# Attention of a three-stage kernel put in order by a list scheduler that models the program fetch

## The chip, the cores and the metric

The kernel runs on one core of a Trainium2 chip. A core has five engines with an instruction stream each: TensorE (PE) for matmuls, VectorE (DVE), ScalarE (ACT), GpSimd (POOL), and SyncE (SP), which here only issues DMAs. Each engine runs its own list in the order in which the program gives it, and waits at an instruction whose inputs or buffers are not ready. The metric is the device time of one execution in microseconds, the median over several runs: 375.57 us before the change (three runs, 374.45 to 375.98).

## The reference

Three layers follow one another. `S` is 576, `D` is 64; there are 4 batches and 8 heads.

```python
scores = scale * (q @ k.T)                        # per batch and head
mask   = local (0 <= i - j < 32)  for heads 0-3
         strided (i >= j, i % 32 == j % 32)  for heads 4-7
attn   = softmax(where(mask, scores, -1e9));  x = attn @ v      # 2304 tokens x 512
logits = x @ phi                                  # 8 experts x 4 slots
d = softmax of logits over tokens;  slot_in = d.T @ x
slot_out[e] = relu(slot_in[e] @ w1[e]) @ w2[e]    # w1 512x1024, w2 1024x512
y   = softmax of logits over slots @ slot_out
out = elu(y @ w_in) @ w_out                       # w_in 512x2048, w_out 2048x512, 8 bytes an element
```

## The kernel before

**Attention.** Both masks leave only small blocks, so attention is done in 20 units. A *local* unit (letter L, twelve of them, in two passes p = 0 and 1 over two heads each) takes a sixth of a pass: one bf16 product that writes the mask into PSUM, 24 small products of keys and queries on top of it, and 12 calls for the values that become 24 matmuls. A *strided* unit (letter S, eight of them, in passes p = 2 and 3) takes a quarter of a pass: a mask product, 32 calls that become 64 matmuls, and 16 calls for the values that become 32. Every matmul has a weight load of its own in front, and both are instructions of PE.

A unit goes through the engines like this: scores on PE (`emit_A`, L172 to L194), maximum and subtraction on DVE (L205, L206), exponential on ACT (`emit_E`, L214), sum, reciprocal, product and transpose on DVE (`emit_N`, L223 to L233), then four copies that spread the transposed blocks into the block-diagonal buffer `bd` (`spread`, L241 on ACT, L243 on POOL, L245 on DVE; the strings of `SPREAD` name the engine of each block), then the value products on PE and their copy to `x_all` on ACT (`emit_PV`, L262 to L281). When all units of a part of the tokens are through, `emit_X` multiplies them by `phi` (L291), transposes them (L298), adds to `logits` on DVE (L301, L303) and copies the transposes back on ACT (L308).

**What sets the order.** `ORDER` gives the sequence of units. A loop over `it` then emits, by hand, the normalisation of unit `it - 1`, the scores of unit `it`, the values of unit `it - 2`, the logits that the table `X_AT` puts there and the loads of the table `LOADS`. After the loop the tail is written out instruction by instruction: the last values, three soft-max steps over tokens (`emit_m`, `emit_mm`, `emit_ex`, `emit_dt`) and the accumulations `emit_acc` of slot inputs. Then come the first expert products (`emit_w1`, L581), the second ones (`emit_w2`, L671) and the MLP, whose operations were already put in order by a list scheduler with due times, written inline.

**Loads and slots.** All loads are issued by SP in program order. There is no room for all weights at once: first weights of experts 0 and 1 go to free slots, the others lie where queries, keys and values were and wait for their last reader. First weight 2 takes the values of pass 2, 3 the strided keys (`kB`), 4 the queries of passes 3 and 0, 5 the values of pass 3, 6 the local values, 7 the local keys (`kA`). Second weights 0 to 2 take `bd` and the two halves of `x_all`, the rest the slots of first weights that were used. `load_head` brings the first 256 columns of `w_in` early.

Of the kernel before, what the change touches and what calls it, by code (L numbers as in the profile page):

```python
# [19 lines left out]
def attn_moe_mlp(ctx, tc, q, k, v_l, v_s, phi, w1, w2, w_in, w_out, out):  # L20
# [18 lines left out]
    ORDER = "LLSLSSLSSLSSLSLLLLLL"  # L39
# [33 lines left out]
    def region(tag, name):  # L73
        return slots.tile([128, SIZE[tag]], F32, tag=tag, name=name)

# [72 lines left out]
    pend_S = []  # L148

# [7 lines left out]
    nth = [sum(y[0] // 2 == x[0] // 2 for y in units[:n]) for n, x in enumerate(units)]  # L157
    st = {}

# [5 lines left out]
    def emit_A(n):  # L165
        p, t, h = units[n]
        qt, kt = qk_t[p]
        if p < 2:
            u = 2 * t + h
            ps = s_ps[n % 2][:, 0:384].rearrange("p (a b) -> p a b", b=64)  # L170
            m0 = 0 if u == 0 else 1
            nc.tensor.matmul(  # L172
                s_ps[n % 2][:, 0:384], ident16, lmask16[:, m0:m0 + 3].rearrange("p i h x -> p (i h x)"),
                start=True, stop=False,
            )
            for j in range(3):
                i = 3 * u + j
                for b in range(B):
                    c0 = 128 * i + 32 * b
                    nc.tensor.matmul(  # L180
                        ps[32 * b:32 * b + 32, 2 * j:2 * j + 2, :], qt[:, c0:c0 + 32], kpair(p, i, b),
                        start=False, stop=(j == 2),
                    )
            s = small("s", 384, "ls", 3, 6, 64)
            ops_ = []
            w = 6
            pa = s
        else:
            ps = s_ps[n % 2][:, 0:16 * MR].rearrange("p (a b) -> p a b", b=MR)
            nc.tensor.matmul(s_ps[n % 2][:, 0:16 * MR], ident16, smask16, start=True, stop=False)  # L190
            for j in range(0, 16, 2):
                for b in range(B):
                    c0 = 576 * h + 288 * (j // 8) + B * MR * (j % 8 // 2) + b * MR
                    nc.tensor.matmul(  # L194
                        ps[32 * b:32 * b + MR, j:j + 2, :], qt[:, 1152 * t + c0:1152 * t + c0 + MR], kt[:, t, :, c0:c0 + MR],
                        start=False, stop=(j == 14),
                    )
            s = small("s", 16 * MR, "ss", 3, 16, MR)
            ops_ = []
            w = 16  # L200
            pa = pst[nth[n] % 2][:, :, 0:MR]
        sh = [128, w, s.shape[2]]
        mx = sl_p.tile([128, 16, 1], F32, tag="mx", name="mx", bufs=3)
        sc = ps
        ops_.append(lambda: nc.vector.reduce_max(out=mx[:, 0:w, 0], in_=sc, axis=AX.X))  # L205
        ops_.append(lambda: nc.vector.tensor_tensor(  # L206
            out=s, in0=sc, in1=mx[:, 0:w].to_broadcast(sh), op=ALU.subtract
        ))
        st[n] = [pa, w, sh, s]
        return ops_  # L210

    def emit_E(n):
        pa, s = st[n][0], st[n].pop()
        nc.scalar.activation(out=pa, in_=s, func=AF.Exp, scale=scale)  # L214

    def emit_N(n):
        p, t, h = units[n]
        pa, w, sh = st[n]
        sm = sl_p.tile([128, 16, 1], F32, tag="sm", name="sm", bufs=4)
        st[n].append(sm)  # L220
        sv = sm[:, 0:w]
        ops_ = [
            lambda: nc.vector.reduce_sum(out=sv[:, :, 0], in_=pa, axis=AX.X),  # L223
            lambda: nc.vector.tensor_scalar(out=sv, in0=sv, scalar1=1e-9, scalar2=None, op0=ALU.add),
            lambda: nc.vector.reciprocal(out=sv, in_=sv),
        ]
        bd = bds[n % 2]
        st[n].append(bd)
        ops_.append(lambda: nc.vector.tensor_tensor(out=pa, in0=pa, in1=sv.to_broadcast(sh), op=ALU.mult))
        r, x = (12, 32) if p < 2 else (16, MR)  # L230
        tr = small("pt", 32 * r, "tr", 2, r, 32)
        pin = pa.rearrange("p a (k x) -> p (a k) x", x=32) if p < 2 else pst[nth[n] % 2]
        ops_.append(lambda: nc.vector.transpose(out=tr, in_=pin))  # L233

        def spread():
            for b in range(B):
                q32 = slice(32 * b, 32 * b + 32)
                o, i = bd[q32, 0:r, 32 * b:32 * b + x], tr[q32, :, 0:x]
                e = SPREAD[1 if p >= 2 else 2 if n == nu - 1 else 0][b]
                if e == "A":  # L240
                    nc.scalar.activation(out=o, in_=i, func=AF.Copy)  # L241
                elif e == "G":
                    nc.gpsimd.tensor_copy(out=o, in_=i)  # L243
                else:
                    nc.vector.tensor_copy(out=o, in_=i)  # L245

        pend_S.append(spread)
        return ops_

    SPREAD = ("GAGA", "AAAA", "GAVA")  # L250
    nu = len(units)

    def emit_PV(n):
        p, t, h = units[n]
        pa, w, sh, sm, pt = st.pop(n)
        if p < 2:
            o = o_ps[nth[n] % 2][:, 0:384].rearrange("p (j x) -> p j x", x=128)
            for j in range(3):
                i = 3 * (2 * t + h) + j
                for k in range(2):  # L260
                    for e in range(2):
                        nc.tensor.matmul(  # L262
                            o[64 * e:64 * e + 64, j, :], v_t[p][:, max(i - 1 + k, 0), e, :], pt[:, 4 * j + 2 * e + k],
                            start=(k == 0), stop=(k == 1),
                        )
            i = 3 * (2 * t + h)
            nc.scalar.activation(out=x_all[:, POS[p], i:i + 3, :], in_=o, func=AF.Copy)
        else:
            xv = x_all[:, POS[p]].rearrange("p m (b q) -> p q b m", b=B)
            for g in range(2):  # L270
                og = ps_t.tile([128, 512], F32, tag="t", name="so")[:, 0:4 * B * MR]
                for j in range(4):
                    c0 = B * MR * j
                    r = 4 * g + j
                    for hh in range(2):
                        nc.tensor.matmul(
                            og[64 * hh:64 * hh + 64, c0:c0 + B * MR], v_t[p][:, t, h, hh, r, :],
                            pt[:, 8 * hh + r].rearrange("p (b m) -> p b m", b=B)[:, :, 0:MR], start=True, stop=True,
                        )
                q0 = 16 * t + 8 * h + 4 * g  # L280
                nc.scalar.activation(  # L281
                    out=xv[:, q0:q0 + 4], in_=og.rearrange("p (j b m) -> p j b m", b=B, m=MR), func=AF.Copy
                )

    seen = set()

    def emit_X(p, t):
        xt = x_all[:, POS[p], 6 * t:6 * t + 6, :]
        lg = ps_l.tile([128, 192], F32, tag="l", name="lg")
        for b in range(B):  # L290
            nc.tensor.matmul(  # L291
                lg[32 * b:32 * b + 32, :], phi_sb[:, p, :], xt[:, :, 32 * b:32 * b + 32], start=True, stop=True
            )
        xps = []
        for g in range(2):
            xps.append(ps_t.tile([128, 3, 128], F32, tag="t", name="xtps"))
            for j in range(3):
                nc.tensor.transpose(xps[g][:, j, :], xt[:, 3 * g + j, :], ident)  # L298
        d = logits[:, 192 * t:192 * t + 192]
        if t not in seen:  # L300
            nc.vector.tensor_copy(out=d, in_=lg)  # L301
        else:
            nc.vector.tensor_tensor(out=d, in0=lg, in1=d, op=ALU.add)  # L303
        seen.add(t)
        if p == 1:
            nc.vector.reduce_max(out=nm3[:, t:t + 1], in_=d, axis=AX.X)
        for g in range(2):
            nc.scalar.activation(out=xt[:, 3 * g:3 * g + 3], in_=xps[g], func=AF.Copy)  # L308

    with tc.manual_schedule():  # L310
# [57 lines left out]
        load_q(0, 0, A0)  # L368
        load_k(0, 0, A0)
        load_v(0, 0, A0)  # L370
# [49 lines left out]
        def at_k(p, x):  # L420
            return lambda: load_k(p, HW_ * x, HW_ * x + HW_)
# [84 lines left out]
        for f in pend_S:  # L506
            f()
# [579 lines left out]
```

## Time and profile before

| what | value |
|---|---|
| median of three runs | 375.57 us (374.45 to 375.98) |
| the profiled execution, its own time | 374.55 us |
| its span, first to last instruction | 372.8 us |
| mean granted TensorE clock | 0.982 |
| PE busy | 344.3 us, 2957 matmuls |
| DVE busy | 262.7 us |
| ACT busy | 246.0 us |
| DMA, whole span | 71.58 MB, mean 192 GB/s |
| chain that ended last | PE 82%, DVE 7%, ACT 4%, POOL 3%, issue 2% |

Busy shares are means over stages with different limits: attention to about 100 us, experts to about 140 us, the MLP after. A row of a timeline has its start, its length, the engine, the line of the code, what is written from what is read, and in brackets how long the engine sat idle before it and who released it. "issue" means that the engine waited for nothing that the profile shows.

### The profile page before, as it was taken

How to read it: one execution, taken by the hardware profiler on the slowest of the kernel's cores; microseconds unless marked ns; L12 is line 12 of the kernel's file. 1: busy time of each engine (PE TensorE's matmuls, PEld its weight loads, DVE VectorE, ACT ScalarE, POOL GpSimd, SP SyncE). 2: the span in 40 equal slices, each digit the busy share in tenths (PEclk: the TensorE clock that was granted, in tenths of full speed). 3: DMA queues.
4: the chain of work that ended last, by engine and by line, in shares of the span. 5: the costliest groups of instructions: out<-in, count | busy, mean ns of one | idle time of the engine just before them, and what ended most of it. 6: DMA issues, size and time to landing. Idle time of an engine off the chain costs nothing.

```text
span 372.8 us, 7425 instructions
## 1 busy us (share of the span) xinstructions
PE 344.3 (92%) x2957; PEld 252.9 (68%) x2957; DVE 262.7 (70%) x535; ACT 246.0 (66%) x482; POOL 25.9 (7%) x60
## 2 busy tenths in 40 slices
PE   7576797798799999999999999999999999999995
PEld 4464565576333337878688778888868888888884
DVE  6778648689261317979999999999854665476741
ACT  5469569767423226999999678868665666666660
POOL 8611011122020000000000000000000000000000
PEclk9699889999999999999999999999999999999999
DMA  7999998996899999755000144100000011033301
GB/s 223 389 414 415 421 419 293 401 413 219 329 413 396 421 408 405 280 225 193 34 1 0 41 186 183 44 1 0 2 0 1 2 56 56 2 113 113 114 0 56
DMA packets 15970, 71.58 MB, mean 192 GB/s; under 512 B 1600, under 2 KB 1856, under 8 KB 11328
## 3 DMA queue, kind: packets, MB, share of 16 engines
q1 hardware_dynamic: 15936, 71.11, 48.9%
q8 instruction: 23, 0.38, 0.4%
q14 instruction: 11, 0.09, 0.1%
HBM read 66.39 MB, written 4.72 MB: 191 GB/s over the span
## 4 chain that ended last, share of the span: by engine, by line
PE 82%; DVE 7%; ACT 4%; POOL 3%; issue 2%; POOLq 0%; ACTq 0%; DVEq 0%
PE ops L939 18%; PE ops L940 18%; PE ops L941 18%; PE hps L897 5%; PE o_ps L671 4%; PE s_ps L581 4%; PE o_ps L262 3%; ACT bd L241 2%; PE xtps L298 2%; PE s_ps L180 2%; DVE tr L233 1%; PE wps L1034 1%; DVE mx L205 1%; PE mps L806 1%; DVE ls L206 1%
## 5 line engine op out<-in xcount | busy, mean ns | idle before, releaser
L907 DVE SCALAR_TENSOR_TENSOR g<-hps,g 128x512 f32<-128x512 f32 (+1 forms) x80 | 50.7, 635 | 19.5 <-ACT g L904 19.4
L901 ACT ACTIVATE g<-hps 128x512 f32<-128x512 f32 (+1 forms) x80 | 44.4, 555 | 20.9 <-PE hps L897 19.4
L904 ACT ACTIVATE g<-g 128x512 f32<-128x512 f32 (+1 forms) x80 | 47.1, 588 | 1.4
L941 PE MATMUL ops<-wh,glo 128*128 128x512 f32 x86 | 33.5, 390 | 0.0
L941 PE MATMUL ops<-w,glo 128*128 128x512 f32 x86 | 33.5, 389 | 0.0
L913 ACT ACTIVATE ghi<-g 128x512 fp32r<-128x512 f32 (+1 forms) x40 | 23.6, 590 | 14.3 <-DVE g L907 12.9
L913 ACT ACTIVATE rings<-g 128x512 fp32r<-128x512 f32 (+1 forms) x40 | 23.5, 588 | 12.4 <-DVE g L907 10.3
L897 PE MATMUL hps<-pers 128*128 128x512 f32 (+1 forms) x80 | 29.3, 372 | 0.0
L939 PE MATMUL ops<-wh,ghi 128*128 128x512 f32 x72 | 28.9, 401 | 0.0
L939 PE MATMUL ops<-wh,rings 128*128 128x512 f32 x72 | 28.8, 400 | 0.0
L241 ACT ACTIVATE bd<-tr 32x288 f32<-32x288 f32 (+1 forms) x56 | 26.8, 479 | 2.7 <-DVE tr L233 1.2
L939 PE MATMUL ops<-w,ghi 128*128 128x512 f32 x72 | 28.5, 395 | 0.0
L940 PE MATMUL ops<-wl,ghi 128*128 128x512 f32 x72 | 28.1, 390 | 0.0
L940 PE MATMUL ops<-w,rings 128*128 128x512 f32 x72 | 28.1, 390 | 0.0
L939 PE MATMUL ops<-w,rings 128*128 128x512 f32 x72 | 28.1, 390 | 0.0
L940 PE MATMUL ops<-w,ghi 128*128 128x512 f32 x72 | 28.1, 390 | 0.0
L940 PE MATMUL ops<-wl,rings 128*128 128x512 f32 x72 | 28.0, 390 | 0.0
L941 PE MATMUL ops<-wh,rings 128*128 128x512 f32 x58 | 22.6, 390 | 0.0
L941 PE MATMUL ops<-w,rings 128*128 128x512 f32 x58 | 22.6, 389 | 0.0
L262 PE MATMUL o_ps<-bd,v 128*64 128x128 f32 x288 | 21.0, 302 | 1.7 <-POOL bd L243 1.7
L262 PEld LDWEIGHTS o_ps<-bd,v 128*64 128x64 f32 x288 | 17.8, 151 | 4.2 <-issue 2.2
L917 DVE TENSOR_TENSOR glo<-g,rings 128x512 fp32r<-128x512 f32 (+1 forms) x24 | 15.2, 634 | 7.2 <-ACT rings L913 4.3
(207 smaller groups left out, 717.9 us busy)
## 6 DMA issues: line engine op xcount, KB each, us to landing
w<-in_moe_w_dram SPq DMA_DIRECT2D x8, 1024.0 KB, 12.2
v<-in_moe_w_dram SPq DMA_DIRECT2D x7, 1024.0 KB, 14.1
w<-in_moe_w_in_dram SPq DMA_DIRECT2D x3, 2048.0 KB, 7.4
out_dram<-ob SPq DMA_DIRECT2D x18, 256.0 KB, 2.0
v<-in_v_s_dram SPq DMA_DIRECT2D x4, 1024.0 KB, 9.8
kB<-in_moe_w_dram SPq DMA_DIRECT2D x4, 1024.0 KB, 12.6
xw<-in_moe_w_dram SPq DMA_DIRECT2D x4, 1024.0 KB, 7.6
xw<-in_moe_w_out_dram SPq DMA_DIRECT2D x2, 2048.0 KB, 7.6
```

Source lines behind the costliest of these rows:

```text
L241: nc.scalar.activation(out=o, in_=i, func=AF.Copy)
L262: nc.tensor.matmul(o[64 * e:64 * e + 64, j, :], v_t[p][:, max(i - 1 + k, 0), e, :], pt[:, 4 * j + 2 * e + k], start=(k == 0), stop=(k == 1),)
L581: nc.tensor.matmul(hp[32 * g:32 * g + 32, :], siT[:, c, :], w_at(2 * a + g // 2, 0, 2 * c + g % 2), start=(c == CO[0]), stop=(c == CO[-1]),)
L897: nc.tensor.matmul(t["ps"], M4[:, 128 * f:128 * f + 128], cTf[:, t0:t0 + n], start=True, stop=True)
L901: nc.scalar.activation(out=t["g"], in_=t["ps"], func=AF.Exp)
L904: nc.scalar.activation(out=t["g"], in_=t["g"], func=AF.Relu, scale=-1.0, bias=1.0)
L907: nc.vector.scalar_tensor_tensor(out=t["g"], in0=t["ps"], scalar=0.0, in1=t["g"], op0=ALU.max, op1=ALU.subtract)
L913: nc.scalar.activation(out=t["hi"], in_=t["g"], func=AF.Copy)
L917: nc.vector.tensor_tensor(out=t["lo"], in0=t["g"], in1=t["hi"].bitcast(F32), op=ALU.subtract)
L939: nc.tensor.matmul(o, t["hi"][:, c], hi, start=(f == f0), stop=False)
L940: nc.tensor.matmul(o, t["hi"][:, c], lo, start=False, stop=False)
L941: nc.tensor.matmul(o, t["lo"][:, c], hi, start=False, stop=(f == f1 - 1))
```

## The change

`ORDER` puts strided and local units mostly in turns. The list scheduler of the MLP becomes a function, `list_order`, with three additions: engines beside the four (GpSimd), pools whose members must be taken in the order of their keys (`fifo`), and a model of PE's fetch: after every 256 instructions PE can go on only 6.25 us after it entered the block before. The loop, the tables `LOADS` and `X_AT` and a part of the tail are replaced by nodes for that function: every operation of a unit, every load of attention and of first weights (and of second weight 0), the logits, and the tail up to the second accumulation. Each node has an engine, a duration, its inputs, a key (3.2 us a unit) and a pool. The operations themselves are those of before, except that the first two units spread all blocks on ACT, the last unit spreads like every local one, and some loads come in two pieces.

```diff
-    ORDER = "LLSLSSLSSLSSLSLLLLLL"
+    ORDER = "LLSLSLSLSLSLSLLSLSLL"
+    MULG = False
+    FIFO = ("sp", "s", "pst", "mx", "sm", "tr", "bd", "o", "t", "l")
+    T0, TP, AE = 6.0, 3.2, 0.1
...
+    def list_order(nodes, pools, eps, free=None, fetch=None, fifo=()):
...
+        def fetched(n, t, commit=False):
+            if not fetch or nodes[n][0] != "P":
+                return t, t + nodes[n][1]
+            size, lat, count, _ = fetch
+            i, left, dur = done[0], count.get(n, 0), nodes[n][1]
+            ent = list(entered)
+            x, c = t, max(left, 1)
+            while left:
+                step = min(left, size - i % size)
+                if i % size == 0:
+                    x = max(x, ent[-1] + lat)
+                    ent.append(x)
+                x += dur * step / c
+                i, left = i + step, left - step
...
+            return t, x if count.get(n, 0) else t + dur
...
+        def start_of(n):
+            eng, dur, deps, key, fn, alloc, at = nodes[n]
+            if alloc:
+                if alloc[0] in fifo and queue[alloc[0]][0] != n:
+                    return 1e9
...
+        while len(order) < len(nodes):
+            best = (1e8,)
+            for e in free:
+                c = [(start_of(n), nodes[n][3], n) for n in ready[e]]
+                if c:
+                    lim = min(c)[0] + eps
+                    x = min((key, t, n) for t, key, n in c if t <= lim)
+                    best = min(best, (x[1], x[2], e))
...
-    SPREAD = ("GAGA", "AAAA", "GAVA")
+    SPREAD = ("GAGA", "AAAA")
...
-        for it in range(nu):
-            m = it - 2
-            na = emit_N(it - 1) if 0 <= it - 1 < nu else []
-            aa = emit_A(it) if it < nu else []
-            for f in na[0:4] + aa + na[4:]:
-                f()
-            emit_E(it)
-            for f in pend_S:
-                f()
-            pend_S.clear()
-            if 0 <= m < nu:
-                emit_PV(m)
-            for x in X_AT.get(it, ()):
-                emit_X(*x)
-            for f in LOADS.get(it, ()):
-                f() if callable(f) else f[0](*f[1:])
...
+        def load_node(kind, p, a, b, after=()):
+            f = {"q": load_q, "k": load_k, "v": load_v}[kind]
+            need = min(users(p, kind, a, b))
+            key = T[need] - (14 if kind != "v" else 9)
+            dur = 128 * 4 * (b - a) / 1e6 * RATE
+            post.append((key, dur, after, lambda: f(p, a, b), (kind, p, a, b)))
...
+        WS = ((0, 0, ()), (1, 8, ()), (2, 1, v_of(2)), (3, 7, q_of(3)), (4, 5, q_of(3, 0)), (5, 2, v_of(3)))
+        for e, s, after in WS:
+            for a, b in (LO, HI):
+                w_node(e, e, s, a, b, after)
...
+            y = qk[n] = an("P", c(1.1, 1.0), deps, K, f_qk, ("sp", rel["sp"]), c(50, 130))
+            y = an("V", c(0.48, 0.4), [y], K + 1.2, f_mx, ("mx", rel["mx"]))
+            y = an("V", c(0.48, 0.4), [y], K + 1.7, f_sub, ("s", rel["s"]))
...
+            y = an("A", c(0.46, 0.39), [y], K + 2.3, f_exp, None if local else ("pst", rel["pst"]))
...
+            for b, e in enumerate("AAAA" if n < 2 else SPREAD[0 if local else 1]):
+                sp.append(an(e, (c(0.45, 0.37) if e == "A" else 0.5), [y] + sp[:1], K + 4.9, f_sp(b, e, b == 0),
+                             None if b else ("bd", rel["bd"])))
...
+                y = an("P", 1.5, sp + vd, K + 6.5, f_pv, ("o", rel["o"]), 48)
...
+        x = an("P", 1.6, [x] + xe[0], KT + 3, f_acc0, ("t", r_acc), 24)
...
+        an("P", 1.6, acc1_deps, KT + 6, lambda: emit_acc(1, acc1, 0, 6), None, 24)
+        order, end = list_order(anodes, apools, AE, dict(A=4.8, V=5.2, G=11.0, P=5.0, S=2.0), (256, 6.25, count, 99), FIFO)
+        for t, n in order:
+            anodes[n][4]()
```

## Rows read from the trace of the kernel before

**Rows 1.** Chain that ended last, in order of time, whole span: start, us, what.
```profile
106.83 7.07 PE s_ps L581 x64
...
138.38 2.07 PE o_ps L671 x16
```
**Rows 2.** Line 415, its issues: duration in ns, first and last start.
```profile
L415 SPq DMA_DIRECT2D q<-in_moe_w_dram x6: 327/328/705, 62.6 to 123.9; - x6
```
**Rows 3.** DMA issues of 122 to 125 us: KB, us to landing.
```profile
q<-in_moe_w_dram SPq DMA_DIRECT2D x1, 512.0 KB, 15.4
```
**Rows 4.** The page: busy time and instructions; the instruction queue.
```profile
PE 344.3 (92%) x2957; PEld 252.9 (68%) x2957; DVE 262.7 (70%) x535; ACT 246.0 (66%) x482; POOL 25.9 (7%) x60
...
q8 instruction: 23, 0.38, 0.4%
```
**Rows 5.** PE in order of time, 30 to 40 us: start, us, instructions.
```profile
31.91 0.98 PE L194 MATMUL s_ps<-kB,q 128*18 128x36 f32 x64
...
38.37 0.38 PE L194 MATMUL s_ps<-kB,q 128*18 128x36 f32 x22 [2.64 <-issue]
```
**Rows 6.** PE in order of time, 50 to 62 us.
```profile
53.27 0.53 PE L194 MATMUL s_ps<-kB,q 128*18 128x36 f32 x39 [0.17 <-issue]
...
59.28 0.47 PE L276 MATMUL so<-bd,v 128*64 128x72 f32 x7 [0.49 <-issue]
```
**Rows 7.** PE's groups, 0 to 100 us: busy, mean ns, idle before.
```profile
L262 PE MATMUL o_ps<-bd,v 128*64 128x128 f32 x288 | 21.0, 302 | 1.7 <-POOL bd L243 1.7
L298 PE MATMUL xtps<-ident,xw 128*128 128x128 f32 x72 | 12.0, 295 | 5.1 <-ACT xw L281 5.1
L276 PE MATMUL so<-bd,v 128*64 128x72 f32 x256 | 11.4, 239 | 5.7 <-ACT bd L241 5.0 <-issue 0.5
L180 PE MATMUL s_ps<-kA,q 128*32 128x128 f32 x288 | 11.1, 290 | 0.4 <-DMA kA<-in_k_dram 0.4
L194 PE MATMUL s_ps<-kB,q 128*18 128x36 f32 x512 | 7.0, 205 | 5.5 <-issue 2.8 <-POOL negm L356 2.7
L291 PE MATMUL lg<-xw,phi 128*32 128x192 f32 x96 | 6.7, 354 | 1.7 <-ACT xw L267 1.7
```
**Rows 8.** DVE by stretch: length, busy (instructions), clock, DMA share, GB/s.
```profile
7.80:91.10 83.30, 62.49 (x153) 0.92 0.97 383
77.56:84.93 7.37, 6.52 (x17) 1.00 0.97 392
```
**Rows 9.** PE in order of time, 5 to 30 and 77 to 100 us.
```profile
12.10 1.17 PE L194 MATMUL s_ps<-kB,q 128*18 128x36 f32 x64 [2.72 <-POOL negm L356]
...
81.17 0.86 PE L180 MATMUL s_ps<-kA,q 128*32 128x128 f32 x24
...
84.86 0.86 PE L180 MATMUL s_ps<-kA,q 128*32 128x128 f32 x24
...
95.24 1.53 PE L262 MATMUL o_ps<-bd,v 128*64 128x128 f32 x24
```
**Rows 10.** ACT in order of time, 84 to 100 us.
```profile
90.78 1.07 ACT L241 ACTIVATE bd<-tr 32x384 f32<-32x384 f32 x2 [0.54 <-DVE tr L233]
```
**Rows 11.** All engines by stretch; the last column is GB/s.
```profile
0.00:10.00 10.00, 6.83 (x67) 4.27 (x67) 6.08 (x11) 5.14 (x8) 8.86 (x25) 1.00 0.70 218
...
90.00:95.00 5.00, 3.52 (x45) 2.40 (x41) 3.39 (x15) 3.09 (x8) 0.62 (x1) 1.00 0.51 162
...
100.00:105.00 5.00, 4.54 (x27) 1.17 (x23) 2.44 (x10) 1.79 (x5) 0.00 (x0) 1.00 1.01 426
```
**Rows 12.** SyncE's issues in order of time, 57 to 126 us.
```profile
58.71 2.33 SPq L415 DMA_DIRECT2D kB<-in_moe_w_dram  x2
...
92.67 4.98 SPq L415 DMA_DIRECT2D bd<-in_moe_w_dram  x2
```
**Rows 13.** DMA issues of 93.5 to 97.65 us: KB, us to landing.
```profile
bd<-in_moe_w_dram SPq DMA_DIRECT2D x1, 1024.0 KB, 4.8
```
**Rows 14.** PE by stretch: length, busy (instructions), granted clock, DMA share, GB/s.
```profile
38.70:41.40 2.70, 2.70 (x30) 0.50 1.01 415
```

More of the change, by code (lines that the diff above doesn't have):

```diff
@@ L212, in emit_E @@
[L212 to L248, printed above, removed]
@@ L250, in attn_moe_mlp @@
-    SPREAD = ("GAGA", "AAAA", "GAVA")
-    nu = len(units)
[L253 to L308, printed above, removed]
+    nu = len(units)
@@ L461, in attn_moe_mlp @@
         dsum = misc.tile([128, 3], F32, name="dsum")
[L462 to L463 removed]
+        acc_sb = []
         dl = {}
@@ new lines, in attn_moe_mlp @@
+        for kind in "qk":
+            load_node(kind, 0, 0, A0)
+        load_node("v", 0, 0, A0)
+        load_node("q", 0, A0, QW)
+        load_node("k", 0, A0, HW_)
+        load_node("k", 0, HW_, QW)
+        load_node("v", 0, A0, QW)
+        for p in (2, 3):
+            for x in range(2):
+                h = (HW_ * x, HW_ * x + HW_)
+                load_node("q", p, *h)
+                load_node("k", p, *h, after=[("qk", n) for n in users(2, "k", *h)] if p == 3 else ())
+                load_node("v", p, 2048 * x, 2048 * x + 2048)
@@ new lines, in attn_moe_mlp, with w_node, head_node @@
+        for x in range(2):
+            h = (HW_ * x, HW_ * x + HW_)
+            load_node("q", 1, *h, after=[("qk", n) for n in users(2, "q", *h)])
+            load_node("k", 1, *h, after=[("qk", n) for n in users(0, "k", *h)])
+            load_node("v", 1, *h)
+        def w_node(i, e, s, a, b, after, second=0):
+            post.append((200.0 + i, 128 * 4 * (b - a) / 1e6 * RATE, after, lambda: load_w(e, second, s, (a, b)), None))
+        def head_node(i, s, after):
+            post.append((200.0 + i, 0.6, after, lambda: load_head(s), None))
@@ new lines, in attn_moe_mlp, with make_loads @@
+        made, evs = set(), {}
+        def make_loads():
+            for i, (key, dur, after, f, what) in enumerate(post):
+                if i not in made and all(x[1] in qk and x[1] in pv for x in after):
+                    made.add(i)
+                    deps = [y for k, n in after for y in ([qk[n]] if k == "qk" else pv[n])]
+                    y = an("S", dur, deps, key, f)
+                    if what:
+                        data.append((y, what))
+        left = {p: {t: [n for n in of[p] if p >= 2 or units[n][1] == t] for t in range(3)} for p in range(4)}
@@ new lines, in attn_moe_mlp @@
+        for n, (p, t, h) in enumerate(units):
+            make_loads()
+            evs[n] = unit_nodes(n)
+            if n == max(of[3]):
+                rm = an("V", 0.2, [qk[m] for m in of[2] + of[3]], T[n] + 30, lambda: nc.vector.tensor_scalar(
+                    out=rmask, in0=e0, scalar1=-1.0, scalar2=-NEG, op0=ALU.add, op1=ALU.mult
+                ))
+            for x in range(3):
+                if left[p][x] and left[p][x][-1] == n:
+                    x_nodes(p, x, [y for m in left[p][x] for y in evs[m]], T[n] + 8.5 + (0 if p < 2 else 2.4 * x))
```

452 lines of the change are left out of this document (302 added, 150 removed).

## The prediction

> **What bounds the kernel now.** I first read the page's line of TensorE (PE) and its queue lines, then the chain that ended last, then PE's groups and its order in time up to 100 us, then the shares of engines and DMA by stretch, and last SyncE's issues with their landing. The whole path is PE's: the chain has the first expert product at 106.83 us and the last group of the second ones at 138.38 us [rows 1], and PE has hardly a gap between them. The MLP behind has an order of its own that this change leaves alone, so it can only be shifted as a whole. What the change can move is the attention stage before 106.83 us, and that is worth no more than the DMA allows behind it: the last piece of the last second-expert weight is issued at 123.9 us and needs 15.4 us [rows 2, 3], so it lands at 139.3 us, and PE uses it in the last quarter of the group at 138.38 us, at about 139.9 us. That is 0.6 us of slack. An earlier end of attention gives time only as far as the weights come earlier too. So there are two clocks to move: PE's own (X) and the DMA's (Y).
>
> **PE's program fetch.** The instruction queue brings 23 packets of 0.38 MB together, 16.5 KB each, and PE has 2957 matmuls and as many weight loads, 5914 instructions: one packet for some 256 [rows 4]. PE stops within a strided score product after 42 of 64 pairs for 2.64 us with no releaser, and goes on at 38.37 us [rows 5]. Counted back 256 instructions (86 there, 64 of the value product before it, 106 of the 130 of the score product at 31.91 us), the block before began 11 pairs into the latter, at 31.91 + 11 x 0.0153 = 32.1 us. So two blocks began 6.3 us apart. The same count fits the next pair of stops, at 53.27 and 59.28 us, 6.0 us apart [rows 6]. I take 6.15 us for a block while the DMA is full; the diff's model has 6.25.
> Up to the last logits there are 288 + 72 + 256 + 288 + 512 + 96 matmuls [rows 7] and a mask product for each of 20 units, 1532 in all, so 3064 instructions, 12.0 blocks, 73.8 us. That is attention's floor on PE. VectorE (DVE) is busy for 62.49 of 83.3 us; where it runs without a gap (the last local units, 84.86 - 81.17 = 3.69 us apart) it shows 6.52 of 7.37 us, 0.885 [rows 8, 9]. So its floor is 62.49 / 0.885 = 70.6 us, just under the fetch's. What is lost now lies in waits between the two: PE sat 5.1 us before transposes, 5.7 us before strided value products and 5.5 us before strided scores [rows 7].
> The Trainium skill, page "Runtime: NRT & Kernel Launch", section "Instruction fetch mechanics", speaks against modelling the fetch at all: it too has the refill in blocks of 256 instructions, but says that crossing into a new one is mostly hidden. By that rule only DVE's floor would hold, and spacing the strided units would serve nothing; the 2.64 us stop contradicts it while the DMA is full.
>
> **The change, part by part.** The arithmetic stays, but for three small things: the first two units spread all four blocks on ScalarE, the last unit's third block goes from DVE to ScalarE, and a few loads are cut in two. I cost these at nothing: four spreads at 0.54 us (two in 1.07, [rows 10]) end about when GpSimd's second does now. Bounds: 1 us either way, from two such spreads.
> *Order of units.* A strided unit has 130 + 64 instructions, a local one 50 + 48, each group of logits 28. In turns, they spread the fetch evenly; now seven strided units stand in the first twelve and six local ones last. From the first strided score product (12.10 us) to the last local one (84.86 us) the kernel spends 17 units at 4.28 us [rows 9]. In the new order there are 2642 instructions between the same two points (8 strided and 9 local score products, 17 units' value products, 8 groups of logits): 10.3 blocks, 63.5 us, 3.73 us a unit. These are the ends: 4.28 (nothing gained) and 3.73 (the floor). I take 3.95, nearer to the floor, because the stretch of local units shows that a list with one engine as its bound runs at that bound; not the floor itself, since every strided unit has a chain over four engines that a fixed order meets early or late. That gives 17 x 0.33 = 5.6 us.
> *Order at the end.* The last value product runs at 95.24 us although its last spread was done at 90.78 + 1.07 = 91.9 us [rows 9, 10]: an accumulation that waits for DVE stands ahead of it. The list places it when it is ready. Bounds 0 and 3.4 us; I take 2.2, as PE's accumulations must run somewhere in the same stretch. X = 5.6 + 2.2 = 7.8 us.
> *Order of loads.* SyncE's loads go into the same list, attention's first, the experts' behind; each still waits for its slot, and what is queued behind it on SyncE waits too. What counts is who frees the slots. First weights 3, 4 and 5 lie where strided keys, queries and values were. The first of them is issued at 58.71 us now [rows 12], since the last strided unit is the fourteenth; in the new order it is the eighteenth. At 3.95 us a unit its score product comes at 12.1 + 15 x 3.95 = 71.4 us. Until then the DMA has some 25.5 MB that need nothing from it, 60 us at 426 GB/s and 5 us of slow start (218 GB/s over the first 10 us, [rows 11]), so it idles some 6 us. What remains is 3 x 2.10 MB, 1.57 MB of weights 6 and 7, and 0.52 MB of heads: 8.4 MB, 19.7 us. So the first weights are in at 71.4 + 1 (issue and start) + 19.7 = 92.1 us.
> Now, the DMA falls to 162 GB/s from 90 to 95 us [rows 11], because the pieces that wait for the last units come one by one. The second issue of second weights starts at 92.67 + 4.98 - 0.33 = 97.3 us and lands 4.8 us later [rows 12, 13], at 102.1 us; at full rate these 2.1 MB are 5.0 us, so their stream begins in effect at 97.1 us. In the new order it begins at 92.1 us: Y = 5.0 us, and half a microsecond of slack behind it. The late strided units are thus the cost of the change: they take the early start of weights 3 to 5 away, which pays only because the stage is shorter.
> **Sum.** The smaller of X = 7.8 and Y + 0.5 = 5.5 us: 5.5 us. The profiled execution took 374.55 us (span 372.8 and 1.75 around it), which would become 369.0. It lies 1.0 us under the median of 375.57, so for the median I predict 370.0 us.
>
> **Rivals.**
> *The late strided units starve the DMA* (slower). Place: the slots that the last strided score product frees. Each microsecond that this comes after 76.4 us (97.1 - 19.7 - 1) moves the second weights and all behind them by one. At today's 4.28 us a unit it is 76.3 us, just no loss; at 4.6 us it is 81.1 us, 4.7 us lost: 380.3 us. For it: after the 2.64 us stop PE's granted clock was 0.50 (1.2 GHz, [rows 14]) and a value product took 2.7 us where one at full clock takes 1.53 [rows 9]; 1.2 us lost so in every second of the 10.3 blocks is 0.35 us a unit. Against it: the 4.28 us hold waits of 16 us in three groups alone that an order can take away.
> *Nothing is left* (within 0.5%). At 4.2 us a unit the stream begins at 95.8 us, 1.3 us gained: 374.3 us. For it: the same slots, and transposes and value products wait for ScalarE in any order. Against it: these waits stand on PE's path now, at places where another unit's product was ready.
> *The floor is met.* At 3.73 us the last strided scores come at 68.0 us and the stream begins at 88.7 us; with all 3.4 us at the end, X = 12.8 and Y + 0.5 = 8.9: 366.7 us. For it: local units run at DVE's bound today. Against it: no strided stretch comes near it.
> *The fetch does not bind when spread.* Then DVE's 70.6 / 20 = 3.53 us a unit holds, the last strided scores come at 65.1 us, and the DMA's bytes alone, 33.9 MB or 80 us behind 5 us of slow start, set the stream at 86 us: 11 us gained, 364.5 us. Against it: two spacings of 6.0 and 6.3 us. This is what the page of the Trainium skill on the runtime would give.
>
> **How the numbers follow.** Forecast (2 to 8 us gained, 367.5 to 373.7) 0.54; floor 0.11; no fetch limit 0.03; nothing left 0.15; slower 0.17. About 0.5%, 1.9 us, is what a measurement of this kernel can tell. Faster by more: 0.54 + 0.11 + 0.03 = 0.68; within: 0.15; slower: 0.17. The range takes in the floor's 366.7, both ends of the small things, and the first part of the slower case: 365 to 378.
>
> **What would show it.** Right: the last strided score product at 70 to 73 us, the first expert product at 99 to 102 us, the DMA full from about 72 us on, no PE stop over 3 us, the MLP's span unchanged. The pitch is wrong if the first and last score products stand more than 4.2 us a unit apart; the DMA step is wrong if the second weights' stream begins before the last slot is free, or if PE waits for weights in the second expert products. The forecast as a whole is wrong if the first expert product comes early and the end does not.

## The result, and the profile after

| | before | after |
|---|---|---|
| median | 375.89 us (374.45 to 379.11, 12 runs) | 372.03 us (369.79 to 374.15, 12 runs) |
| ratio, 95% interval | | 0.9896 (0.9865 to 0.9927) |
| profiled execution | 374.55 us | 373.04 us |
| its span | 372.8 us | 371.2 us |
| first expert product | 106.83 us | 104.38 us |
| MLP's first output product | 149.07 us | 147.76 us |

The change gains 3.9 us between the medians, where 5.5 was forecast. The two profiled executions lie nearer together, 1.5 us apart: the one of before is 1.3 us under its median, the one of after 1.0 us over its own. So a trace can place some 1.5 us of the gain, and the timed ratios have to carry the rest.

PE in order of time in the kernel after (start and length in us, line, instructions, idle time before): the first and last score products, the three stops without a releaser, and the tail.

```profile
11.76 0.74 PE L509 MATMUL s_ps<-kB,q 128*18 128x36 f32 x64 [1.16 <-DMA kB<-in_k_dram]
...
32.50 0.66 PE L585 MATMUL so<-bd,v 128*64 128x72 f32 x14 [1.15 <-issue]
...
44.94 0.26 PE L509 MATMUL s_ps<-kB,q 128*18 128x36 f32 x8 [1.77 <-issue]
...
57.62 0.52 PE L656 MATMUL lg<-xw,phi 128*32 128x192 f32 x4 [1.91 <-issue]
...
72.10 0.75 PE L509 MATMUL s_ps<-kB,q 128*18 128x36 f32 x64
...
75.75 1.03 PE L499 MATMUL s_ps<-kA,q 128*32 128x128 f32 x24
...
81.33 0.53 PE L656 MATMUL lg<-xw,phi 128*32 128x192 f32 x8 [2.56 <-ACT xw L592]
...
89.97 1.53 PE L572 MATMUL o_ps<-bd,v 128*64 128x128 f32 x24
91.43 1.91 PE L377 MATMUL acc<-xw,d_loc 128*32 128x512 f32 x12
...
96.24 1.91 PE L377 MATMUL o_ps<-xw,d_loc 128*32 128x512 f32 x12
...
99.97 1.05 PE L377 MATMUL s_ps<-xw,d_loc 128*32 128x512 f32 x4 [1.38 <-DVE dw L761]
...
138.09 1.05 PE L893 MATMUL o_ps<-q,h1T_c 128*32 128x512 f32 x4 [0.23 <-DMA q<-in_moe_w_dram]
```

Against [rows 9]: the last strided scores stand at 72.10 us, forecast 71.4. From the first strided to the last local scores the pitch is (75.75 - 11.76) / 17 = 3.76 us, near the forecast's floor of 3.73. The longest stop is 1.91 us instead of 2.64 [rows 5]; 12.44 and 12.68 us lie between them, two blocks of 6.2 to 6.3. Each time 255 matmuls with as many weight loads stand in between, two short of two times 256 instructions. Then the gain melts. The last value product is 5.3 us earlier (89.97 against 95.24), the first expert product only 2.45: two groups of logits and both accumulations still stand behind that value product, and the last maxima (98.15 us) wait behind them. In the kernel before, the last maxima and what follows them:

```profile
100.54 0.44 PE L481 MATMUL s_ps<-ident,nm 128*128 128x128 f32 x2
100.91 1.05 PE L500 MATMUL o_ps<-xw,d_loc 128*32 128x512 f32 x4
102.42 1.05 PE L500 MATMUL s_ps<-xw,d_loc 128*32 128x512 f32 x4 [0.46 <-DVE dw L539]
```

SyncE's issues in order of time in the kernel after (start, time from the first issue of the row to the end of its last, target); and what SyncE waited for at the weight loads (us in total, times, longest).

```profile
51.03 0.33 SPq L326 DMA_DIRECT2D v<-in_moe_w_dram  x1
68.97 0.33 SPq L326 DMA_DIRECT2D kA<-in_moe_w_dram  x1
70.89 0.33 SPq L326 DMA_DIRECT2D v<-in_moe_w_dram  x1
...
76.09 12.83 SPq L326 DMA_DIRECT2D v<-in_moe_w_dram  x3
88.98 0.42 SPq L326 DMA_DIRECT2D kA<-in_moe_w_dram  x1
```
```profile
SPq L326 <- PE s_ps L499: 15.5, 1, 15.5
```

All engines by stretch in the kernel after: length, busy time and instructions of PE, weight loads, DVE, ACT and GpSimd, granted clock, DMA share, GB/s.

```profile
65.00:70.00 5.00, 4.13 (x91) 3.36 (x86) 4.69 (x13) 4.66 (x10) 1.76 (x4) 1.00 0.10 26
```

The last piece of the first weights: its issue with KB and us to landing after, then its issue in order of time and its landing before.

```profile
kA<-in_moe_w_dram SPq DMA_DIRECT2D x1, 1024.0 KB, 8.1
```
```profile
92.15 0.33 SPq L415 DMA_DIRECT2D v<-in_moe_w_dram  x1
```
```profile
v<-in_moe_w_dram SPq DMA_DIRECT2D x1, 512.0 KB, 3.8
```

SyncE stands for 15.5 us behind a weight piece that waits for late local scores, and the DMA falls to 26 GB/s from 65 to 70 us. Before, the hole was at 90 to 95 us [rows 11]: it moved more than it closed. The last of the first weights is issued at 88.98 us and needs 8.1 us, so it is in at 97.1 us and not at the 92.1 us of the forecast; before, it was in at 92.15 + 3.8 = 96.0 us.

The chain that ended last in the kernel after: start, us, what.

```profile
104.38 3.71 PE s_ps L803 x32
...
109.95 13.03 DMA w<-in_moe_w_dram
123.00 15.05 DMA q<-in_moe_w_dram
138.09 1.05 PE o_ps L893 x4
```

Where the chain was PE's from 106.83 to 138.38 us [rows 1], it now runs through two weight transfers. PE waits for the last second weight, so of 2.45 us 1.31 are left at the MLP's first product.

### The profile page after: what moved, and what is told of

It is laid out like the page before. It is cut to its first block, busy times and chain, and to the rows that moved or that the text cites. A ratio compares the mean times of both kernels' runs of the same rounds, so it can differ in the third digit from the quotient of the medians.

```text
span 371.2 us, 7426 instructions
## 1 busy us (share of the span) xinstructions
PE 344.6 (93%) x2957; PEld 253.8 (68%) x2957; DVE 257.9 (69%) x534; ACT 247.8 (67%) x486; POOL 24.7 (7%) x57
## 4 chain that ended last, share of the span: by engine, by line
PE 76%; DMA 9%; DVE 5%; ACT 4%; issue 2%; POOL 1%; SPq 1%; POOLq 0%; ACTq 0%
PE ops L1161 18%; PE ops L1162 18%; PE ops L1163 18%; PE hps L1119 5%; DMA q<-in_moe_w_dram 4%; DMA w<-in_moe_w_dram 4%; PE xtps L665 3%; PE o_ps L572 3%; ACT bd L559 2%; DMA kA<-in_k_dram 2%; PE so L585 2%; PE lg L656 2%; PE s_ps L499 1%; PE wps L1216 1%; PE mps L1028 1%
## 5 line engine op out<-in xcount | busy, mean ns | idle before, releaser
L559 ACT ACTIVATE bd<-tr 32x288 f32<-32x288 f32 (+1 forms) x60 | 28.7, 479 | 5.2 <-DVE tr L549 3.6
L572 PE MATMUL o_ps<-bd,v 128*64 128x128 f32 x288 | 19.3, 288 | 1.3 <-ACT bd L559 0.9
L572 PEld LDWEIGHTS o_ps<-bd,v 128*64 128x64 f32 x288 | 16.8, 145 | 3.0 <-issue 2.2
```

The lines of the kernel that those rows point to most:

```text
L572: nc.tensor.matmul(o[64 * e:64 * e + 64, j, :], v_t[p][:, max(i - 1 + k, 0), e, :], pt[:, 4 * j + 2 * e + k], start=(k == 0), stop=(k == 1),)
```

## The experiments

Two theories stood after the result. The first, *two clocks* (theory A): PE's attention and the weights' stream both set the expert stage, so a change pays only where both come earlier; what limits the change is the tail on PE and the hole in the loads. The rival, *the turns and the fetch*: the even spread of the strided units is what gains, and the rest is noise of the tail. All ratios are to the kernel before, run on the same chip; its own median was between 375.89 and 377.05 us there, so kernels from different chips are compared by ratio. The four columns on the right are from each kernel's one trace: the profiled execution's own time, the first expert product, the time from there to the MLP's first output product, and the mean GB/s from 20 to 140 us. Where the profiled time is far from the median, the trace speaks for that execution more than for the kernel.

| kernel | median us | ratio (95%) | profiled us | expert starts | to MLP | GB/s |
|---|---|---|---|---|---|---|
| before | 375.89 | 1 | 374.55 | 106.83 | 42.24 | 382 |
| after | 372.03 | 0.9896 (0.9865 to 0.9927) | 373.04 | 104.38 | 43.38 | 389 |
| list, old order | 371.44 | 0.9880 (0.9837 to 0.9922) | 370.76 | 103.44 | 42.04 | 396 |
| loop, new order | 382.35 | 1.0155 (1.0116 to 1.0193) | 383.59 | 114.29 | 43.81 | 358 |
| no fetch model | 375.08 | 0.9970 (0.9943 to 0.9997) | 377.01 | 105.65 | 46.10 | 379 |
| finer loads | 371.33 | 0.9873 (0.9828 to 0.9918) | 371.47 | 102.95 | 43.30 | 394 |
| maxima first | 373.87 | 0.9921 (0.9891 to 0.9950) | 371.88 | 101.83 | 44.81 | 392 |
| finer loads, maxima first | 370.30 | 0.9836 (0.9797 to 0.9875) | 369.47 | 102.02 | 42.25 | 401 |
| before, tail by hand | 374.28 | 0.9948 (0.9920 to 0.9975) | 373.33 | 105.54 | 42.30 | 386 |
| old order, maxima first | 371.15 | 0.9850 (0.9813 to 0.9887) | 372.54 | 101.26 | 46.00 | 395 |
| loads of the model | 374.12 | 0.9936 (0.9912 to 0.9959) | 374.48 | 104.43 | 44.80 | 385 |
| loads without model | 375.43 | 0.9958 (0.9931 to 0.9985) | 374.83 | 103.72 | 45.87 | 382 |
| finer, maxima, old order | 371.02 | 0.9862 (0.9828 to 0.9896) | 371.12 | 102.47 | 43.41 | 395 |
| finer, maxima, again | 370.62 | 0.9863 (0.9814 to 0.9912) | 369.14 | 101.60 | 42.33 | 402 |

From the MLP's first output product to the end of the span the kernels need 223.4 to 223.7 us: the MLP is only shifted.

**The list with the old order of units.**
```diff
-    ORDER = "LLSLSLSLSLSLSLLSLSLL"
+    ORDER = "LLSLSSLSSLSSLSLLLLLL"
```


> The changed kernel with the unit order of before; list scheduler, loads and tail stay. Theory A (two clocks: the end follows the later of PE's chain and the weights' DMA): the strided units are early again, so the slots of first weights 3 and 4 come free near 58 us and the DMA has no hole between 62 and 71 us, but PE's program fetch stops come in the strided stretch and the local units at the end run at DVE's bound, so the last value product stays near 93 to 95 us: 373 to 375 us, ratio to before 0.993 to 0.998. Rival B (the gain is the list's alone, the turns of local and strided units do nothing): as the changed kernel, 372 us, 0.990.

It is as fast as the change (0.9880 and 0.9896). Its rival B, that the gain is the list's alone, came true here, and the 0.993 to 0.998 of theory A did not. PE and DMA in this kernel:

```profile
11.62 0.96 PE L509 MATMUL s_ps<-kB,q 128*18 128x36 f32 x64 [2.54 <-DMA kB<-in_k_dram]
...
83.15 0.86 PE L499 MATMUL s_ps<-kA,q 128*32 128x128 f32 x24
...
91.93 1.53 PE L572 MATMUL o_ps<-bd,v 128*64 128x128 f32 x24 [0.79 <-ACT bd L559]
```
```profile
65.00:70.00 5.00, 4.72 (x83) 3.33 (x83) 4.26 (x10) 3.89 (x9) 1.00 (x2) 0.84 1.01 415
...
90.00:95.00 5.00, 3.63 (x54) 2.75 (x51) 1.03 (x3) 2.48 (x6) 0.93 (x2) 1.00 0.70 247
```

Its scores stand (83.15 - 11.62) / 17 = 4.21 us apart, 0.45 more than in the change, and its value products still end only 2 us later. Its slots come free early, so 65 to 70 us is full, and its hole stays where it was before, but shallower (247 GB/s instead of 162). The pitch of the score products is thus not what sets the stage.

**The new order in the old loop**, with the entries of `LOADS` moved by hand to where the slots come free and those of the logits (`X_AT`) to where their units are through; the placing is mine, so this is not the price of the order alone.
```diff
-    ORDER = "LLSLSSLSSLSSLSLLLLLL"
+    ORDER = "LLSLSLSLSLSLSLLSLSLL"
...
-            13: ((load_w, 3, 0, 7), (load_head, 7), (load_w, 4, 0, 5), (load_head, 5)),
+            17: ((load_w, 3, 0, 7), (load_head, 7), (load_w, 4, 0, 5), (load_head, 5)),
...
-        X_AT = {10: ((2, 0),), 11: ((2, 1),), 13: ((2, 2),), 16: ((3, 0),), 17: ((3, 1),), 19: ((3, 2),)}
+        X_AT = {10: ((2, 0),), 11: ((2, 1),), 13: ((2, 2),), 19: ((3, 0), (1, 0), (3, 1), (3, 2))}
...
```


> The kernel before, its loop and its tail, with the new unit order alone; entries of the two tables are moved to the first step at which their slot is free. Theory A: the loop's pitch stays near 4.3 us a unit, the strided slots come free at about 77 us, four groups of logits fall on the end: 378 to 382 us, ratio 1.006 to 1.018. Rival B: 375 to 377 us, about 1.000. Rival C (the turns alone bring the gain): 372 us.

It is slower, as the slower rival of the prediction and theory A had it: the loop does not hurry the strided units, and the slots come late.

```profile
76.74 0.75 PE L194 MATMUL s_ps<-kB,q 128*18 128x36 f32 x64
...
101.42 2.54 PE L262 MATMUL o_ps<-bd,v 128*64 128x128 f32 x24
```
```profile
65.00:70.00 5.00, 4.74 (x89) 3.58 (x91) 4.62 (x11) 3.56 (x8) 0.00 (x0) 1.00 0.02 7
70.00:75.00 5.00, 3.88 (x126) 2.95 (x122) 4.54 (x12) 4.32 (x9) 1.99 (x4) 1.00 0.02 3
```

The last strided scores stand at 76.74 us, just past the 76.4 us that the rival named as its point, and the DMA idles for 10 us. By the rival's sum 0.3 us past that point would cost 0.3 us; 6.0 are lost (382.35 against 376.32 on that chip). The value products end later by 6.2 us too (101.42 against 95.24), so the loss is not the stream's alone, and how it divides is not shown.

**The list without the fetch model.**
```diff
-        order, end = list_order(..., (256, 6.25, count, 99), FIFO)
+        order, end = list_order(..., None, FIFO)
```


> The changed kernel with the fetch model taken out of the scheduler; order of units as changed. Theory A: the list puts score products too early on PE, the stops at the block boundaries stay 6.0 to 6.3 us apart and now hold operations that others wait for: 0.5 to 3 us over the changed kernel, 372.5 to 375, ratio 0.991 to 0.998. Rival D (the fetch is hidden when the work is spread, the model costs nothing and brings nothing): 371.5 to 372.5, ratio 0.990.

Nearly the whole gain goes, as theory A expected (0.9970 against 0.9896, intervals apart). But its reason fails: PE's last value product stands at 89.65 us, 0.3 us earlier than in the change. What is late is the stream. SyncE in this kernel, in order of time, then what it waited for:

```profile
51.40 17.81 SPq L326 DMA_DIRECT2D kB<-in_moe_w_dram  x2
69.26 0.91 SPq L326 DMA_DIRECT2D q<-in_moe_w_dram  x2
...
71.47 17.13 SPq L326 DMA_DIRECT2D v<-in_moe_w_dram  x5
```
```profile
SPq L326 <- PE s_ps L509: 17.0, 1, 17.0
```

Without the model the list believes that the strided units end earlier, and puts a weight that waits for the last strided scores ahead of pieces that could go. The expert stage then takes 46.10 us against 42.24 before: some 2.7 us of it PE waits for second weights, and 1.1 us are a low clock (last section). The profiled execution is 1.9 us over the median, so these numbers are larger than what the median lost. This suggested that the model pays through the order of the loads.

**Loads of one list, engines of the other.** The list is drawn up twice, with the model and without; SyncE takes its order from one, the engines theirs from the other.
```diff
...
+        work = [n for t, n in listed(None) if anodes[n][0] != "S"]
+        loads = [n for t, n in listed((256, 6.25, count, 99)) if anodes[n][0] == "S"]
...
```


> The list is drawn up twice; the engines take their order from the list without the fetch model, and SP alone takes its order of loads from the list with it. Theory that the model pays by where SP's loads stand: as the change itself, ratio 0.987 to 0.992, TensorE waits for the last second-layer weight under 1 us, and the MLP's first product stands near 147.8 us. Rival that the model pays by the order of TensorE's groups around the stops: as without the model, ratio 0.995 to 0.999, and the MLP's first product stands past 149 us although the loads stand as in the change.

and the mirror image:
```diff
...
+        work = [n for t, n in listed((256, 6.25, count, 99)) if anodes[n][0] != "S"]
+        loads = [n for t, n in listed(None) if anodes[n][0] == "S"]
...
```


> The mirror image: the engines take their order from the list with the fetch model, and SP alone takes its order of loads from the list without it. Theory that the model pays by where SP's loads stand: as without the model, ratio 0.994 to 0.999, SP waits some 17 us in one piece for the last strided scores, and TensorE waits 3 to 5 us for the last second-layer weights. Rival that it pays by the order of TensorE's groups: as the change itself, ratio 0.987 to 0.992.

The mirror came out as the first theory expected: 0.9958, and SyncE stands in one piece for the strided scores. The other half did not: 0.9936 lies between the two windows, and its MLP starts at 149.23 us, as the rival had it. First the mirror's waits, then two stretches of the kernel with the model's loads.

```profile
SPq L326 <- PE s_ps L509: 19.0, 1, 19.0
```
```profile
65.00:70.00 5.00, 3.83 (x165) 2.70 (x167) 4.97 (x14) 2.78 (x6) 1.00 (x2) 1.00 0.39 110
70.00:75.00 5.00, 5.00 (x90) 3.84 (x89) 4.27 (x14) 3.88 (x9) 1.27 (x2) 1.00 0.40 127
```

The same order of loads has a longer hole behind engines that run in another order, since each slot is freed at another time; the first expert product stands where it does in the change (104.43), the MLP's 1.5 us later. So neither half alone keeps the model's 2.8 us (0.9970 - 0.9896 of 376 us); the interval of the first half (0.9912 to 0.9959) still reaches into that of the change, the mirror's does not. That loads and engines have to come from one forecast is my reading and not shown; how much of the 2.8 us is each one's is not settled.

**Finer loads**: first weights 3, 4 and 5 in pieces that wait only for the units that read their part of the slot.
```diff
...
+                3: ((*LO, [("qk", n) for n in p3h0]), (*HI, q_of(3))),
+                4: ((0, 1024, [("qk", n) for n in p3h0]), (2304, 4096, q_of(0)), (1024, 2304, q_of(3, 0))),
+                5: ((*LO, [("pv", n) for n in p3h0]), (*HI, v_of(3))),
...
```


> The changed kernel; first weights 3, 4 and 5 are loaded in pieces, each of which waits only for the units that read its own columns (half of 3, 4 and 5 no longer wait for the last strided unit). Theory A: the DMA's hole between 65 and 70 us (26 GB/s) closes, the second weights come 4 to 6 us earlier, the wait of PE for the last second weight goes, and PE's chain, first expert product near 104 us, sets the end: 1 to 2.5 us gained, 369.5 to 371, ratio 0.983 to 0.987. Rival E (PE's chain alone sets the end already): 372, 0.990.

**Maxima first**: the last maxima ahead of the second accumulation.
```diff
-        an("P", 1.6, acc1_deps, KT + 6, lambda: emit_acc(1, acc1, 0, 6), None, 24)
...
         emit_mm(2)
+        emit_acc(1, acc1, 0, 6)
```


> The changed kernel; at the tail the product for the third token part's maxima stands ahead of the second accumulation (1.9 us on PE) instead of behind it, so that ACT's and DVE's steps run beside the accumulation. In the trace of the changed kernel PE waits 1.38 us for them. Theory A (two clocks, about level in the changed kernel): first expert product 1.4 us earlier, but PE then waits longer for the last second weight: 0 to 0.7 us gained, ratio to before 0.988 to 0.990. Rival E (PE's chain alone): 1.4 us, 370.6, 0.986.

**Both.**

> The changed kernel with both edits: weights 3 to 5 in pieces that wait only for their own readers, and the maxima ahead of the second accumulation. Theory A: both clocks are moved, so the gains add and more: 2 to 3 us under the changed kernel, 369 to 370, ratio 0.980 to 0.984. Rival E (PE alone): 1.4 us, 0.986. Rival F (the DMA alone): as the pieces alone, 0.987.

The clean pair is maxima first without and with finer loads, on one chip. Both start the expert products as early (101.83 and 102.02 us), yet the times are 373.87 and 370.30 us, with intervals apart: with an early PE the loads set the end, as the two clocks have it. Without finer loads PE waits in the second products, and the stage takes 44.81 us:

```profile
135.67 1.05 PE L892 MATMUL o_ps<-q,h1T_c 128*32 128x512 f32 x4 [0.24 <-DMA q<-in_moe_w_dram]
...
136.96 1.05 PE L892 MATMUL o_ps<-q,h1T_c 128*32 128x512 f32 x4 [0.24 <-DMA q<-in_moe_w_dram]
```

Against the change the edits are less clear. Maxima first starts the expert products 2.55 us earlier; 1.45 of it are the edit's, counted from the last value product (104.38 - 89.97 = 14.41 us in the change, 101.83 - 88.87 = 12.96 here), the rest is this execution's. It gains nothing: 0.9921, slower than both theories expected. Finer loads alone close the hole (405 GB/s from 65 to 70 us), and PE waits for no last weight, but the 0.7 us of median are inside the intervals and 0.9873 lies between the two expectations; in the profiled execution a low clock cost PE 2.7 us there (last section). Both together have the lowest median, 370.30 us, as theory A expected. But their interval overlaps that of the change (0.9797 to 0.9875, 0.9865 to 0.9927), and the repetition below gives 0.9863: that both edits beat the change is likely and not shown. PE at the end of attention and at the second products, then the DMA, with both:

```profile
95.47 0.49 PE L354 MATMUL s_ps<-ident,nm 128*128 128x128 f32 x2
95.89 1.91 PE L377 MATMUL o_ps<-xw,d_loc 128*32 128x512 f32 x12
...
133.50 2.14 PE L898 MATMUL o_ps<-q,h1T_c 128*32 128x512 f32 x16
```
```profile
65.00:70.00 5.00, 4.54 (x87) 3.60 (x84) 4.72 (x14) 4.71 (x10) 1.12 (x2) 1.00 0.94 359
```

The last group of second products runs in one piece again (x16, no wait), and no hole is left where the change has 26 GB/s.

**The tail by hand, in the kernel before**: the last value product moved ahead of the accumulation.
```diff
         emit_PV(nu - 2)
+        emit_PV(nu - 1)
...
         emit_acc(0, acc0, 0, Q0)
-        emit_PV(nu - 1)
```


> The kernel before, its loop and order, with one edit of the tail: the last value product is emitted ahead of the maxima and the first accumulation instead of behind them. Theory A (the prediction's term for the end): the product moves from 95.2 to about 92 us, the block-diagonal buffer comes free 3 us earlier and with it the second weights: 1.5 to 2.5 us gained, ratio 0.993 to 0.996. Rival G (what the list gains, it gains in the body of the stage): within 0.5 us, 0.999 to 1.001.

```profile
91.67 2.84 PE L262 MATMUL o_ps<-bd,v 128*64 128x128 f32 x48
```

The last two value products run together from 91.67 us, and 2.0 us are gained (376.24 to 374.28), half of what the change gains, with one line moved and neither list nor turns. From the last local scores to the first expert product the traces have 106.83 - 84.86 = 21.97 us before and 105.54 - 85.74 = 19.80 here. That is the 2.2 us of the forecast's step on the order at the end.

**Maxima first with the old order.**

> List scheduler with the unit order of before (which measured 0.988) and the maxima ahead of the second accumulation. Here the DMA has no hole before the last unit, so by theory A PE's chain is the later clock by a little: 0.7 to 1.4 us under the same kernel without the edit, 370 to 370.7, ratio 0.984 to 0.986. Rival F (the DMA alone): 0.988.

The first expert product comes at 101.26 us, the earliest of all, and the expert stage takes 46.00 us, among the longest. The ratio, 0.9850, is what theory A expected, but its interval overlaps that of the old order without the edit (0.9837 to 0.9922), and the profiled execution is the longest of its six. So whether the edit gains anything here is open. Against maxima first with the turns, on the same chip, the old order is faster (0.9850 and 0.9921, intervals just apart): while the loads wait in large pieces, the turns cost.

**Both edits with the old order, and the best version again** on the same chip.

> The best version so far (list with the model, finer loads, maxima ahead of the second accumulation) with the order of units of before. Theory that the turns bring something as soon as the loads no longer wait in one piece for the last strided scores: slower than the best version by 1 to 3 us (ratio to before 0.987 to 0.992), the stretch from 80 to 95 us below 300 GB/s, and less moved between 20 and 140 us than the 48.1 MB of the best version. Rival that the turns bring nothing in any case: within 0.5 us of the best version (0.982 to 0.986) and 48 MB moved.

> The best version once more, with its own turns of units, on the same chip as the version with the old order, so that the two are compared directly. Both theories: 0.982 to 0.986 of before.

This was to ask whether the turns are worth something once the loads no longer stand still. The medians, 371.02 and 370.62, say 0.4 us, less than their intervals tell and what the rival expected; the first theory's 0.987 to 0.992 was missed (0.9862). In the profiled pair the version with turns is 1.9 us ahead at the MLP (143.93 against 102.47 + 43.41 = 145.88 us) and moves 402 GB/s against 395, as the first theory had it. But its profiled execution, 369.14 us, is 1.5 us under its median, and the other one is at its own. So it stays open: between nothing and 2 us.

## Why the prediction was right, and where it was not

**Direction and bound.** Faster by more than 0.5% held (1.0%, interval 0.7 to 1.4), and so did the frame: two clocks, the smaller of which counts. Finer loads under maxima first show it: PE as early, 3.6 us less. The MLP behind was shifted and not changed. But both terms of the sum were too large: X was 2.45 us and not 7.8, and of Y's 5.0 us nothing was there at the point where the forecast read it, the end of the first weights (97.1 us). By the forecast's own sum that is 0.5 us. The 3.9 us that were timed lie in its range by other ways than it described, and that is partly luck. What the small things cost that it put at nothing, two units' spreads on ScalarE and the loads in two pieces, was not tried alone.

**Order of units, 5.6 us: the failed step.** The pitch was forecast at 3.95 us and measured 3.76, better still, yet the same list with the old order and 4.21 us is as fast. I read a stage's length off its score products. Behind the last of them stand value products, evictions, spreads and logits that do not follow their pitch: in the change PE idles 2.56 us for ScalarE at 81.33 us, and from the last scores to the last value product it needs 89.97 - 75.75 = 14.2 us, with the old order 91.93 - 83.15 = 8.8. Running the scores ahead piled the rest up behind them: between the first strided and the last local scores PE has 1283 matmuls in the change, 1357 with the old order. The other 74, 148 instructions with their weight loads, come later in the change; by 6.15 us for 256 that is an estimated 3.6 us of the 17 x 0.45 = 7.7 us by which the pitch is better.

**Order at the end, 2.2 us: right in the kernel before.** 2.0 by hand. But X was not 7.8: the expert's start moved 2.45 us. What the value products gained was paid back because logits and both accumulations stood between them and the last maxima, 98.15 - 89.97 = 8.2 us, where the kernel before needs 100.54 - 95.24 = 5.3. The forecast had taken that stretch as fixed. It also missed that the change runs each accumulation in one piece: the kernel before keeps a third of the second one (100.91 us) behind the last maxima and then waits 0.46 us; the change has nothing to put there and waits 1.38.

**Order of loads, 92.1 us: wrong by 5.0 us.** The last strided scores were forecast within 0.7 us; what failed is the count of bytes behind them. I let 25.5 MB run ahead of those scores without asking who frees each slot. Beside the 1.57 MB of weights 6 and 7 that I had counted as late, as much again waits for late local units (issued at 68.97 and 70.89 us); SyncE works in order, so it stood 15.5 us at the first of these pieces. Later a piece for the slot of the values held it until 88.9 us, with the last piece of weight 7 behind it (88.98). By the numbers, 1.57 MB at 426 GB/s are 3.7 us and the scores were 0.7 us late; 0.6 us are left unplaced. The first weights were in at 97.1 us, 1.1 us later than before. What the MLP gained came further down the stream: from 95 to 100 us the DMA moves 419 GB/s, before 297, and the last second weight landed at 123.00 + 15.05 = 138.1 us instead of 139.3.

**Late strided units cost the change: half right.** In the loop the new order costs 1.55%, though not by the stream alone. In the change SyncE stands first for late local scores (15.5 us); finer loads fill that hole with pieces that had waited for strided units. And with maxima first the turns cost 0.7% against the old order.

**The fetch.** The stops came as counted, 6.2 to 6.3 us a block, none over 3 us. The Trainium skill's sentence ("Runtime: NRT & Kernel Launch", "Instruction fetch mechanics") that the crossing is mostly hidden does not agree with stops of 1.15, 1.77 and 1.91 us, here again while the DMA is full. The measurement decides. But the stops are not what the gain is made of: without the model PE's value products ended no later.

**The size.** In the end 5.5 us was forecast and 3.9 measured. The tail's order alone is worth 2.0 in the kernel before; that the same 2.0 are in the change is argued and not shown, since its tail pays 2.9 back. The rest, about 2, the list gives with the old order of units as well. For it no single place is shown: the intervals of the kernel with the tail by hand (0.9920 to 0.9975) and of the list with the old order (0.9837 to 0.9922) only just touch.

## What to carry to other kernels

Where a stage ends in weights that follow through reused slots, forecast two clocks, and for the loads ask for each piece who frees its slot and what stands behind it on the issuing queue: one piece that waits holds all of them. Don't read a stage's rate off its first operation; read it off the last one that the next stage needs. And before a scheduler is credited, move by hand the one operation that is plainly late.

## What the runs showed that was not expected

In three kernels (no fetch model, loads without it, finer loads) the granted clock was low in the first expert product and just ahead of it, in their profiled runs. PE from there to the end of the first 32 expert products in the change, then with finer loads, and the stretch of the latter:

```profile
101.26 1.06 PE L377 MATMUL s_ps<-xw,d_loc 128*32 128x512 f32 x8
...
102.99 1.08 PE L789 MATMUL sip<-e,acc_sb 128*128 128x32 f32 x8 [0.34 <-DVE acc_sb L781]
...
104.38 3.64 PE L803 MATMUL s_ps<-w,siT 128*32 128x512 f32 x32
```
```profile
98.17 1.86 PE L377 MATMUL s_ps<-xw,d_loc 128*32 128x512 f32 x8
...
100.67 1.92 PE L795 MATMUL sip<-e,acc_sb 128*128 128x32 f32 x8
...
102.95 4.70 PE L809 MATMUL s_ps<-w,siT 128*32 128x512 f32 x32
```
```profile
100.00:105.00 5.00, 4.90 (x27) 2.56 (x28) 2.92 (x6) 0.22 (x1) 1.89 (x3) 0.50 0.91 369
```

That is 1.2 instead of 2.4 GHz. The first 32 expert products took 4.66 to 4.77 us in the three, 3.64 in all others, and the way to them from the wait for the last maxima 1.6 to 1.7 us more. So 2.7 us of PE's path went that way in each; it tells in the time where PE is the later clock, as with finer loads, where no last weight was waited for. In the stretch before, 95 to 100 us, PE was busy for 3.62 of 5 us in the change, at full clock behind it, and for 3.62 in the kernel with loads without the model, where the clock fell: its busy time there does not tell which of the two happens.

The runs of one kernel spread over 2 to 5 us (369.79 to 374.15 after), so a single profile of either kernel can lie 1 us or more from its median. Which part of the program varies was not tried.
